# Conformer block on one core: the passage from attention over batch norm to FF2 rebuilt, softmax sums taken as one row, weight fold moved later

## Chip, cores, metric

One core of one Trainium2 chip. The metric is the time of one execution in device microseconds. Most runs of a kernel agree within 0.3%. Spans are from the profiled execution, which is about 4 us shorter than the time of the same execution (2103.5 against 2107.25 us).

Names: PE is TensorE, DVE is VectorE, ACT is ScalarE, POOL is GpSimd, SP is SyncE, whose queue issues most transfers. SBUF is the on-chip memory, PSUM the memory that matmuls write. FF1 and FF2 are the two feed-forward parts of the reference, pw1 and pw2 the products with `w_pw1` and `w_pw2`; the gate is `a * _sigmoid(b)`, swish is `_silu`. Warm matmuls are dummies whose result nobody uses; they run to keep PE's clock full.

## The reference, cut

```python
B, T, D, K = (2, 4000, 512, 3); F = 4 * D
h = _layernorm(x);  x1 = x + 0.5 * (_silu(h @ w_ff1_a) @ w_ff1_b)
h = _layernorm(x1); q, k, v = h @ w_q, h @ w_k, h @ w_v
p = _softmax(einsum('btd,bsd->bts', q, k) * scale)
x2 = x1 + einsum('bts,bsd->btd', p, v) @ w_o
h = _layernorm(x2) @ w_pw1; a, b = h[..., :D], h[..., D:]
h = a * _sigmoid(b)
dc = three-tap convolution of h along T, per channel
mu, var = mean and variance of dc over ALL B*T rows, per channel
dc = (dc - mu) / sqrt(var + 1e-05)
x3 = x2 + _silu(dc) @ w_pw2
x4 = x3 + 0.5 * (_silu(_layernorm(x3) @ w_ff2_a) @ w_ff2_b)
return _layernorm(x4)
```

The batch statistics need every row before any row can go on. That is the narrow place between attention and FF2: little work is ready there, and PE must be kept from standing still.

## The kernel before

The 8000 rows are 16 chunks of 500, each of 4 tiles of 125. Everything is kept in SBUF, bf16. PSUM is four S banks and four Y banks, each taken in turn. A helper records each operation and puts in the semaphore waits; engines work strictly in program order. `after(n, f)` runs f n steps later in the emission; one step is one block of FF1 or FF2, or one key tile in attention. Scores use M = Wq Wk^T and the output Wvo = Wv Wo, both computed once (the "fold") between FF1 matmuls. Attention is two matmul groups per key tile, scores (into S) and values (into Y), with values four tiles behind. The convolution of chunks 0 to 12 is done by DVE beside attention; chunks 13 to 15 come after it, as three diagonal matmuls ("depthwise").

The end of an attention chunk:

```python
def finish_queries(self, b, qc, done):          # called after the chunk's last value group
    for dc in range(DC):                        # clear the four Y banks: DVE 1, 3; ACT 0, 2
        ...
    S.op("DVE", ... tensor_copy(self.ahi, self.acc[s]))            # split of the f32 exp sums into two bf16 parts, hi ...
    S.op("DVE", ... tensor_tensor(out=self.alo, in0=self.acc[s], in1=self.ahi, op=ALU.subtract))  # ... and lo
    def sums():
        ps, b_ps = self.sbank()
        for ti in range(TPC):                   # 8 matmuls with ONE column each
            for part, bp in ((self.ahi, self.b_ahi), (self.alo, self.b_alo)):
                self.mm(ps[0:TILE, ti:ti + 1], part[:, ti * TILE:(ti + 1) * TILE], self.onec[:, 0:1], ...)
        S.op("DVE", ... reciprocal(self.rl[s], ps[0:TILE, 0:TPC]))
    self.after(1 if last else 2, sums)          # then 4 projections, residual by DVE with rl as scalar
```

The fold and its check (the flag says whether scores are bounded, so that exp needs no row maximum):

```python
self.after(6, self.fold_weights)                # counted from block 8 of FF1's first chunk
def fold_weights(self):
    ...                                         # 8 groups of 4 matmuls, one group per step
    def bound():
        S.op("DVE", ... tensor_reduce(self.nr1, self.nrm, AX.X, ALU.add))
        self.mm(ps[0:1, 0:1], self.nr1, self.onef, ...)      # PE waits for DVE here
        ...
    self.after(10, bound)
```

The passage, shortened: gate of chunk 14 and the last projections by steps; layer norm of chunk 15 with transposes by DMA; gate of 15 with depthwise 13 to 15; batch scale for all four channel blocks at once; twelve weight loads for FF2 from ACT's queue; then swish and pw2 of four chunks, each pw2 tile followed by a DVE residual, with the layer norm of chunk 0 in DVE's order after the first chunk; then FF2.

## Time and profile before

| | before |
|---|---|
| time, median of 4 (range) | 2109.22 us (2107.47 to 2110.82) |
| span of the profiled run | 2103.5 us |
| start to first attention group (q of the next chunk) | 461.13 us |
| from there to the last value groups ("the mark") | 1089.90 us |
| mark to first FF2 matmul | 66.83 us |
| first FF2 matmul to end | 485.64 us |

The four pieces add up to the span and are read from PE's timeline.

### The profile page before, as it was taken

What the parts mean: (1) busy time and instruction counts of PE and PEld (TensorE: products, weight loads), DVE (VectorE), ACT (ScalarE), POOL (GpSimd) and SP (SyncE); (2) the same over time, 40 slices, a digit from 0 to 9 for tenths busy, and PEclk for the clock granted to TensorE, in tenths of its full rate; (3) what the DMA queues carried; (4) which work ended last, traced back from release to release, by engine and by line L of the source; (5) the groups of instructions that cost most, each with busy time, mean ns of one, the idle gap of its engine ahead of it and who ended that gap; (6) DMA issues with size and microseconds to landing.
All of it is one profiled execution on the core that took longest, in us unless ns stands there. A gap on an engine that the chain in (4) does not pass through costs nothing.

```text
span 2103.5 us, 24444 instructions
## 1 busy us (share of the span) xinstructions
PE 2063.4 (98%) x9708; PEld 1040.7 (49%) x9710; DVE 1092.4 (52%) x2235; ACT 733.8 (35%) x1251; POOL 124.0 (6%) x260
## 2 busy tenths in 40 slices
PE   8999999999999999999999999999987999999998
PEld 4555555554444444444444444444443555555554
DVE  3345444324556566656665666566755344444433
ACT  3333333333333333333333333333325334434332
POOL 0111100000000000000000000000000000000000
PEclk9999999999999999999999999999999999999999
DMA  6222221110000000005300000000134011111111
GB/s 169 60 55 57 60 61 52 45 43 11 11 11 8 18 18 18 11 15 121 75 11 16 17 18 11 18 16 18 49 97 119 23 38 33 30 40 30 33 38 41
DMA packets 197262, 84.83 MB, mean 40 GB/s; under 512 B 145812, under 2 KB 196631, under 8 KB 197143
## 3 DMA queue, kind: packets, MB, share of 16 engines
q1 hardware_dynamic: 190567, 78.84, 15.2%
q10 hardware_dynamic: 6576, 4.38, 0.7%
q8 instruction: 78, 1.28, 0.3%
q14 instruction: 41, 0.34, 0.1%
HBM read 29.53 MB, written 19.04 MB: 23 GB/s over the span
## 4 chain that ended last, share of the span: by engine, by line
PE 94%; DVE 3%; SPq 1%; DMA 1%; ACT 1%; issue 0%; ACTq 0%; POOL 0%; POOLq 0%; DVEq 0%
PE s L458 54%; PE y L458 40%; DVE work L787 1%; SPq L491 1%; DVE work L792 1%; DMA xt<-in_x_dram 1%; DVE work L749 0%; ACT work L483 0%; DVE work L522 0%; DVE work L545 0%; DVE work L791 0%; ACTq L487 0%; SPq L487 0%; DMA keys<-in_w_o_dram 0%; POOL work L532 0%
## 5 line engine op out<-in xcount | busy, mean ns | idle before, releaser
L483 ACT ACTIVATE work<-s 128x500 bf16<-128x500 f32 (+2 forms) x1062 | 623.0, 587 | 1250.5 <-PE s L458 1240.4
L458 PE MATMUL s<-work,wff 128*128 128x500 bf16 x2560 | 629.8, 377 | 4.0 <-DVE wff L831 3.4
L458 PE MATMUL y<-work,keys 128*128 128x500 bf16 x2048 | 519.1, 374 | 1.2
L458 PE MATMUL s<-work,keys 128*128 128x500 bf16 x2048 | 517.4, 374 | 0.1
L458 PE MATMUL y<-wff,work 128*125 128x512 bf16 x2016 | 506.6, 379 | 0.0
L749 DVE TENSOR_TENSOR work<-work 128x500 f32<-128x500 f32 x496 | 334.7, 675 | 304.6 <-ACT work L483 302.8
L458 PEld LDWEIGHTS s<-work,wff 128*128 128x128 bf16 x2560 | 250.4, 98 | 284.1 <-DVE wff L831 3.9
L458 PEld LDWEIGHTS y<-wff,work 128*125 128x125 bf16 x2016 | 275.2, 137 | 173.5
L458 PEld LDWEIGHTS y<-work,keys 128*128 128x128 bf16 x2048 | 198.0, 97 | 244.3 <-DVE work L787 15.5
L458 PEld LDWEIGHTS s<-work,keys 128*128 128x128 bf16 x2048 | 199.2, 98 | 228.9 <-DVE work L678 0.6
L591 DVE SCALAR_TENSOR_TENSOR xt<-y,xt 125x512 bf16<-125x512 f32 x128 | 79.7, 682 | 369.2 <-PE y L458 369.2
L522 DVE BATCH_NORM_STATS2 work<-xt 125x6 f32<-125x512 bf16 x320 | 201.6, 679 | 9.4 <-DMA xt<-in_x_dram 9.3
L458 PE MATMUL s<-work 128*125 128x512 bf16 (+3 forms) x666 | 150.2, 349 | 22.2 <-DVE work L792 7.9
L532 POOL TENSOR_TENSOR work<-work 125x4 f32<-125x4 f32 x79 | 84.3, 1067 | 1147.9 <-DVE work L530 1147.9
L545 DVE TENSOR_SCALAR work<-xt,work 125x512 bf16<-125x512 bf16 x288 | 115.6, 447 | 21.5 <-POOL work L532 18.8
L458 PEld LDWEIGHTS s<-work 128*125 128x125 bf16 (+2 forms) x666 | 82.8, 137 | 76.5 <-issue 12.2
L591 DVE SCALAR_TENSOR_TENSOR xt<-s,xt 125x512 bf16<-125x512 f32 x64 | 43.7, 690 | 134.5 <-PE s L458 134.5
L831 DVE SCALAR_TENSOR_TENSOR wff<-wff,s 128x500 bf16<-128x500 f32 x64 | 43.2, 677 | 63.1 <-PE s L458 63.1
L483 ACT ACTIVATE wff<-s 128x500 f32<-128x500 f32 x64 | 37.6, 587 | 79.7 <-PE s L458 75.2
L591 DVE SCALAR_TENSOR_TENSOR xt<-s,work,xt 125x512 bf16<-125x512 f32 x64 | 48.1, 751 | 33.1 <-PE s L458 32.2
L458 PE MATMUL s<-keys,work 128*128 128x500 bf16 x256 | 64.4, 376 | 0.0
L483 ACT ACTIVATE work<-keys,work 128x500 bf16<-128x500 bf16 x64 | 49.6, 794 | 5.9 <-DMA wff<-in_w_ff_a_dram 3.7
(61 smaller groups left out, 420.8 us busy)
## 6 DMA issues: line engine op xcount, KB each, us to landing
xt<-in_x_dram SPq DMA_DIRECT2D x15, 500.0 KB
out_dram<-work SPq DMA_DIRECT2D x15, 500.0 KB
dcvd<-wff SPq DMA_DIRECT2D x52, 125.0 KB, 1.7
keys<-dcvd SPq DMA_DIRECT2D x13, 500.0 KB, 5.1
keys<-work SPq DMA_DIRECT2D x8, 512.0 KB, 3.6
keys<-keys SPq DMA_DIRECT2D x32, 128.0 KB, 2.3
work<-work SPq DMA_TRANSPOSE x188, 2.5
wff<-in_w_ff_a_dram SPq DMA_DIRECT2D x8, 256.0 KB, 5.3
```

What stands on the lines that cost most here:

```text
L458: self.S.op("PE", lambda e: e.matmul(out, lhsT, rhs, start=start, stop=stop), reads=reads, writes=[bank], inc=stop if inc is None else inc)
L483: return self.S.op("ACT", lambda e: e.activation(out, in_, func, **kw), reads=reads, writes=writes)
L491: return self.S.dma("SP", k, lambda e: e.dma_start_transpose(dst, src), reads=reads, writes=writes)
L522: self.S.op("DVE", lambda e: e.bn_stats(self.st[sl][:, ti, :], self.XT[g]), reads=[self.bx[g]], writes=[self.b_st[sl][ti]])
L532: S.op("POOL", lambda e: e.tensor_tensor(out=self.rs[sl], in0=self.va[sl], in1=self.neghalf[0:TILE, :], op=ALU.pow), reads=[self.b_va[sl], ...
L545: self.S.op("DVE", lambda e: e.tensor_scalar(out, self.XT[g], self.mv[sl][:, ti, 0:1], self.rs[sl][:, ti:ti + 1], ALU.subtract, ALU.mult), ...
L591: self.S.op("DVE", lambda e: e.scalar_tensor_tensor(out=self.XT[g], in0=ps, scalar=scalar, in1=self.XT[g], op0=ALU.mult, op1=ALU.add), rea ...
L749: S.op("DVE", lambda e, p=p: e.tensor_tensor(out=self.acc[s], in0=self.acc[s], in1=self.P[p], op=ALU.add), reads=[self.b_P[p], self.b_acc[ ...
L787: S.op("DVE", lambda e, dc=dc: e.tensor_copy(self.OT[:, dc, :], self.Yb[dc][:, 0:CHUNK]), reads=[self.b_Y[dc]], writes=[self.b_OT[dc]])
L792: S.op("DVE", lambda e: e.tensor_tensor(out=self.alo, in0=self.acc[s], in1=self.ahi, op=ALU.subtract), reads=[self.b_acc[s], self.b_ahi], ...
L831: self.S.op("DVE", lambda e: e.scalar_tensor_tensor(out=self.G[gs][:, jj, 1:1 + CHUNK], in0=self.th[k], scalar=1.0, in1=ps[:, 0:CHUNK], op ...
```

## The change

Five intentions: (1) sums as one row, with the split of the sums done before the last value groups; (2) fold later, so that its weights have landed; (3) ten more warm-up matmuls; (4) the passage reordered: gate of chunk 14 on ACT and POOL, PE transposes in place of DMA transposes, batch scale per channel block, residual of two chunks as an identity matmul on PE, 16 warm matmuls, FF2 loads from SP; (5) three instead of four chunks of pw2 ahead of FF2.

```diff
+                if kt == TB - 1:
+                    self.split_sums(s)              # ahi, alo: before the 4 lagging value groups
...
+    def sum_row(self, s):
+        ps, b_ps = self.sbank()
+        for part, bp in ((self.ahi, self.b_ahi), (self.alo, self.b_alo)):
+            self.mm(ps[0:1, 0:CHUNK], self.onec[:, 0:1], part, ...)      # 2 matmuls, 500 columns
+        self.act(self.row, ps[0:1, 0:CHUNK], AF.Copy, [b_ps], [self.b_row])
+        self.store(self.rowd[s:s + 1, :], self.row, ...)                 # row to DRAM
+        ... dma_start(self.sq[s], self.rowd[s].rearrange("(t p) -> p t", p=TILE))   # and back as columns
+        self.after(5, ... reciprocal(self.rl[s], self.sq[s]))
+    def finish_queries(self, g, done):
+        self.copy_o()
+        if g == NCK - 1: return
+        self.sum_row(g % 2)
...
     def conv_a(self, t, jj):
+        if t == NCK - 2:
+            self.act(asb, ps[:, 0:CHUNK], AF.Copy, [b_ps], [b_asb], scale=2.0)
+            self.S.op("POOL", ... tensor_tensor(out=out, in0=asb, in1=self.th[k], op=ALU.mult))
+        elif t == NCK - 1:
+            self.S.op("DVE", ... scalar_tensor_tensor(out=out, in0=ps[:, 0:CHUNK], scalar=2.0, in1=self.th[k], ...))
...
+    def pw2_sum(self, t, tiles, banks):
+            self.mm(ps[0:TILE, :], self.ident[0:TILE, 0:TILE], self.XT[g], True, False, ...)   # residual on PE
+            ... four pw2 matmuls ...
+            self.act(self.XT[g], ps[0:TILE, :], AF.Copy, [b_ps], [self.bx[g]])
...
-        self.warm(20)
+        self.warm(30)
-            self.after(6, self.fold_weights)
+            self.after(18, self.fold_weights)
...
+        self.sums_direct(last % 2)              # last chunk: the eight short matmuls
+        for ti in range(TPC):                   # gate groups of 14 between the projections of 15
+            gate.pop(0)(); self.project(last, ti); self.ln_stats(last, sl, ti)
+        self.ln_aggr(last, sl)
+        while gate: gate.pop(0)()
+        ... norms on DVE; self.transposes_pe(1, ("DVE", "DVE")); depthwise, gate of 15 interleaved
-            self.load_wa(i["w_ff2_a"], k, "ACT")
+            self.load_wa(i["w_ff2_a"], k)
-        AHEAD = 4
+        AHEAD = 3
+        self.warm(16)
+        ... pw2(0) with DVE residual; pw2_sum(1), pw2_sum(2); transposes of chunk 0 by PE
```

## The prediction

> **What bounds the kernel now.** I read the page first, then the waits of TensorE (PE), then the timeline in the three places where those waits sit.
>
> ```profile
> span 2103.5 us, 24444 instructions
> PE 2063.4 (98%) x9708; PEld 1040.7 (49%) x9710; DVE 1092.4 (52%) x2235; ACT 733.8 (35%) x1251; POOL 124.0 (6%) x260
> ...
> PE 94%; DVE 3%; SPq 1%; DMA 1%; ACT 1%; issue 0%; ACTq 0%; POOL 0%; POOLq 0%; DVEq 0%
> ```
>
> PE is the bound: 98% busy, and 94% of the chain that ended last. Only time in which PE does no useful matmul can be won. How much is that? In the last stretch of attention, 39 groups of four 128x500 matmuls start between 1516.36 and 1549.34 us: 32.98/156 = 0.2114 us per matmul. A chunk of FF1 (64 such matmuls and 64 of 125x512) repeats every 27.415 us, which leaves 0.217 us for a 125x512. The groups of the page hold 6948 of the first kind and (adding the 32 FF2 and 2 fold records that are missing) 2624 - 32 = 2592 of the second: 1468.8 + 562.5 = 2031 us. With the start (12.4 us before the first FF1 matmul) and the end (5.8 us after the last matmul) that makes 2050 us. Some 54 us of the 2103.5 are loss, more than the 40 us of PE idle, because a stalled or slowly clocked matmul counts as busy. No view shows a second place to win from.
>
> Loss one, in every attention chunk (timeline of the kernel before, PE, DVE):
>
> ```profile
> 1428.87 1.25 DVE L787 CAST work<-y 128x500 bf16<-128x500 f32 x2
> 1429.15 1.42 PE L458 MATMUL y<-work,keys 128*128 128x500 bf16 x4
> 1430.05 0.41 DVE L791 CAST work<-work 128x500 bf16<-128x500 f32 x1
> 1430.48 0.68 DVE L792 TENSOR_TENSOR work<-work 128x500 bf16<-128x500 f32 x1
> 1430.51 0.22 PE L458 MATMUL s<-work 128*125 128x1 bf16 x1
> 1431.22 0.56 PE L458 MATMUL s<-work 128*125 128x1 bf16 x7 [0.49 <-DVE work L792]
> 1431.64 1.01 PE L458 MATMUL s<-work,keys 128*128 128x500 bf16 x4
> ```
>
> A group of four takes 0.85 us elsewhere. Here the next chunk's first value group waits for VectorE (DVE) to clear the Y banks (starts 1429.15, next start 1430.51: 1.36), then the eight one-column sums wait for the hi/lo split that DVE does after those copies (0.71 + 0.42). Extra: 1.36 + 0.71 + 0.42 - 0.85 = 1.64 us. Check: a steady chunk repeats every 69.42 us and holds 304 x 0.2114 + 16 x 0.217 = 67.74, which leaves 1.68.
>
> Loss two, the weight fold in FF1's first chunk:
>
> ```profile
> 35.18 1.03 PE L458 MATMUL y<-wff,work 128*125 128x512 bf16 x4
> 37.43 0.81 PE L458 MATMUL s<-keys 128*128 128x512 bf16 x3 [1.22 <-DMA keys<-in_w_k_dram]
> ...
> 41.67 1.02 PE L458 MATMUL s<-keys 128*128 128x512 bf16 x4 [1.72 <-DMA keys<-in_w_o_dram]
> ```
>
> The fold waits for its weights, 1.22 + 1.72 = 2.9 us. Before that, at 12.4 to 15.3 us, seven FF1 matmuls come 0.42 apart: slow clock after the idle start, about 1.5 us.
>
> Loss three, the passage from attention to FF2:
>
> ```profile
> 1551.03 3.53 PE L458 MATMUL y<-work,keys 128*128 128x500 bf16 x16
> ...
> 1571.02 1.22 PE L458 MATMUL s<-work,wff 128*128 128x500 bf16 x4 [3.40 <-DVE wff L831]
> ...
> 1597.78 9.76 PE L458 MATMUL s<-work 128*125 128x512 bf16 x32 [7.67 <-ACT work L483]
> 1610.93 7.09 PE L458 MATMUL s<-work 128*125 128x512 bf16 x32 [3.39 <-DVE xt L591]
> 1617.86 4.41 PE L458 MATMUL s<-work,wff 128*128 128x500 bf16 x20
> ```
>
> From 1551.03 to the first FF2 matmul at 1617.86 are 66.8 us for 120 x 0.2114 + 80 x 0.217 + 0.4 = 43.2 us of matmuls. Loss: 23.7 us. The three long waits are layer norm of chunk 15 on DVE; batch statistics, the ACT table and twelve weight loads issued from ScalarE's own queue ahead of the first swish; and layer norm of chunk 0 standing in DVE's order ahead of a residual that holds a bank. Slow clock after each wait is the rest.
>
> **What the Trainium skill says.** "TensorE: Matmul & The Clock Gate", Part 1: a warm matmul starts every N/2.4 ns + about 2.5, i.e. 210.8 and 215.8 ns for 500 and 512 columns (measured here 211.4 and 217), and the clock halves after an idle window of some 3.4 us and comes back after a busy one. The trace agrees: 20 dummy matmuls ended at 7.4 us, FF1 began slowly at 12.4 and was fast from 15.28. "ScalarE: Activation LUTs", Table sets: exp and tanh share a set, sigmoid anchors another; a load is 1283 ns. The trace has three loads of 1283 ns, none between Exp and Tanh; the change adds one. "GPSIMD Engine Reference", 3.1: a two-input elementwise instruction takes about 2.6 cycles per element at 1.2 GHz. My estimate for 500 elements is 1.1 us and dispatch; the trace before has no such instruction. "DMA: Bandwidth & Descriptors", Anatomy of one DMA: about 2 us fixed per transfer (its fit is for another queue). Here 125 KB to DRAM landed in 1.7 us.
>
> **The change part by part.**
>
> *Sums as one row (15 of 16 chunks).* The split moves to the end of the chunk, before the four lagging value groups, so DVE has done it 6 us early. Eight one-column matmuls become two of 500 columns: 2 x 0.2114 = 0.42 us. These also stand between the last value group and the next chunk's first, so the Y copies get that much more time: the fourth matmul would now start at about 1430.2, and the copies above ended at 1430.12; the 0.5 us stall of the Y group shrinks to about 0. Gain per chunk 1.64 - 0.42 - 0.03 = 1.19; x15 = 17.8 us. The round trip of the row through DRAM (ScalarE copy 0.6, store about 2, load of 500 four-byte elements 3 to 4) ends roughly 7 us after the sums; its reciprocal is issued five steps later, about 7.9 us. If DVE waits there 1 or 2 us it costs nothing: DVE is busy 43.7 of 69.4 us per chunk, and eight P buffers and four S banks give it several us.
>
> *Later fold.* Same 32 matmuls, weights long landed: 2.9 us won. *Ten more warm matmuls* run at 0.21, to 9.5 us instead of 7.4, in idle time; whether they hold the clock until 12.4 depends on the window: half of 1.5, 0.7 us.
>
> *Passage.* I rescheduled it by hand from the durations above (DVE 0.6 to 0.75 per residual, stats or gate; ScalarE 0.59 per copy, 0.72 per swish; pow 1.0).
> - To 1554.4 values, sums 0.5, last values to 1555.8, gate group to 1556.65, projection waits 0.4 for the O copies; seven more groups alternate gate and projection to 1563.0; four gate groups to 1566.4. ScalarE and GpSimd take gate 14, so DVE is free: residual, stats, aggregate, pow end at 1566.3, norms follow. The 3.4 us wait becomes about 0.3.
> - Sixteen PE transposes paced by the norms to 1568.1, six depthwise matmuls to 1569.4 under their DVE copies. That replaces transposes by DMA.
> - Gate 15 and depthwise 13 to 15: 62 matmuls, 13.1 us, to 1582.5. DVE has about 15 us here (4 gates, 12 stats of 0.65, 4 aggregates of 0.6) and then the last scale chain: shift at 1587.0. Swishes run 1586.0 to 1591.7 because ScalarE's copies precede them. The 16 warm matmuls cover to 1586.
> - pw2 of chunk 0 ends at 1591.0 (pace of the swishes); chunks 1 and 2 with the residual as an identity matmul, 40 x 0.217 = 8.7, to 1599.6; layer norm of chunk 0 (DVE, done 1598.6) is hidden; transposes 1.4 and an eviction: FF2 starts at 1601.9.
>
> So 1617.9 - 1601.9 = 16.0 us; but pw2 of chunk 3 now runs inside FF2: 16 x 0.217 = 3.5 back. Net 12.5; I take 1 off for waits that I didn't see: 11.5.
>
> Sum: 17.8 + 2.9 + 0.7 + 11.5 = 32.9. From 2110.19: 2077.3, so 2077.
>
> **Rivals.**
> - *The row's round trip becomes the wait.* It is a chain of two dependent transfers of tiny elements. If it took 12 us rather than 7, DVE would stand 4 us in front of the residuals and the exp sums, P buffers would run out, and PE would lose perhaps 1 us per chunk: about 2092. For it: SyncE's queue is in order and carries the conv stores. Against: at that point the trace shows that queue free, and stores landing in 1.7 us.
> - *The passage stays bound by DVE and ScalarE.* The passage had only 40.0 us DVE and 26.2 us ScalarE in 66.9, so neither fills it, but between gate 15 and swish DVE is the longer one even in my schedule. A slow GpSimd multiply (3 us), or a cold clock for two windows, takes 3 to 6 us: about 2082.
> - *It gains as much as there is.* PE work of the new passage, with transposes, identity and warm matmuls, is 47.5 us: FF2 at 1598.5. With all of the 1.5 us at the start: 2071. So 2% (2068) is beyond what I can find to remove.
>
> **Range and chances.** Attention is 15 repeats of one well-read wait (17.8, give or take 2); passage 11.5, give or take 4; start 3.6, give or take 1; the three runs before spread over 3.4 us. Together 2069 to 2086. Faster by over 2% would need everything and the noise: 0.07. Slower by 2% needs a new wait of over 70 us: 0.01. Within 2%: 0.92.
>
> **What would show it.** Steady chunks every 68.2 us instead of 69.4, with two 128x500 matmuls where the eight were, no DVE release there; no DMA release in the first 60 us; first FF2 matmul 51 us, give or take 4, after the mark from which 66.8 were counted above, no wait over 2.5 us in the passage. I am wrong if reciprocals wait long for their DMA and PE follows, if DVE or ScalarE still leaves PE over 4 us idle ahead of pw2, or if the chunk period stays at 69.

## The result

| | before | after | gain | predicted |
|---|---|---|---|---|
| median of 4 | 2109.22 | 2080.02 (2079.44 to 2083.02) | ratio 0.9865 [0.9848, 0.9882] | 2077 |
| span | 2103.5 | 2076.1 | 27.4 | 32.9 |
| start to attention | 461.13 | 460.71 | 0.4 | 3.6 |
| attention to mark | 1089.90 | 1074.29 | 15.6 | 17.8 |
| mark to FF2 | 66.83 | 51.91 | 14.9 | 15 (16.0 less 1) |
| FF2 to end | 485.64 | 489.19 | -3.5 | -3.5 |

Two rows were missed: the start gave almost nothing, and attention gave 2.2 us less. The passage came as predicted in sum. The gain is clear of the noise but under 2%, the least that counts here as faster.

The page of the kernel after, engine totals and the chain that ended last (shares by engine):

```profile
PE 2060.9 (99%) x9684; PEld 1040.1 (50%) x9686; DVE 1088.8 (52%) x2235; ACT 748.5 (36%) x1282; POOL 126.7 (6%) x267
...
PE 97%; DVE 1%; ACT 0%; issue 0%; DMA 0%; POOL 0%; POOLq 0%; SPq 0%
```

PE is still the bound, more than before. Its waits (line, for whom, total us, times, longest):

```profile
PE s L467 <- DVE work L1053: 2.8, 1, 2.8
PE s L483 <- DVE work L560: 2.4, 3, 1.2
PE s L467 <- ACT work L498: 2.0, 4, 0.8
PE s L467 <- DVE work L1071: 1.7, 1, 1.7
PE s L467 <- DVE work L490: 0.6, 1, 0.6
```

The 16 waits for the split, the two for the fold's weights and the 7.7 us ahead of swish are gone. One is new and the longest: 2.8 us for line 1053, which is the `tensor_reduce` of the bound check. The sums in attention (timeline after, PE and DVE):

```profile
1413.50 1.00 PE L467 MATMUL y<-work,keys 128*128 128x500 bf16 x4
1414.43 0.58 PE L467 MATMUL s<-work 128*1 128x500 bf16 x2
1414.95 1.02 PE L467 MATMUL s<-work,keys 128*128 128x500 bf16 x4
1415.81 1.00 PE L467 MATMUL y<-work,keys 128*128 128x500 bf16 x4
...
1423.99 0.17 DVE L837 RECIPROCAL work<-work 125x4 f32<-125x4 f32 x1
```

The value group at 1415.81 runs through in 1.00 instead of 1.42 us and no DVE wait is left, as predicted. The reciprocal starts without a wait, in all 15 chunks, so the trip through DRAM is hidden. But from value group to value group (1413.50 to 1415.81) are 2.31 us against the usual 1.69: the row costs 0.62, not 0.45. The period is 68.39 us (1414.43 to 1482.82), 1.03 less than before, and 15 x 1.03 = 15.5.

The passage (timeline after, PE, the starts of its stages):

```profile
1535.00 3.54 PE L467 MATMUL y<-work,keys 128*128 128x500 bf16 x16
...
1551.26 1.03 PE L483 MATMUL s<-work 125*128 125x125 bf16 x12 [1.20 <-DVE work L560]
1553.16 0.38 PE L483 MATMUL s<-work 125*128 125x125 bf16 x4 [0.87 <-DVE work L560]
...
1572.01 0.40 PE L467 MATMUL s<-work 128*125 128x512 bf16 x1 [0.70 <-ACT work L498]
...
1586.91 3.35 PE L467 MATMUL s<-work,wff 128*128 128x500 bf16 x15 [0.81 <-ACT work L498]
```

No wait is over 1.2 us where there had been 3.4, 7.7 and 3.4. But from 1567.8 to 1572.0 PE runs only the 16 warm matmuls and then waits 0.7 us: 4.2 us without useful work, until ScalarE's swishes come (PE idled 7.7 us there before). So the prediction's second rival, a passage still bound by DVE and ScalarE, holds in part; its schedule had counted on such a stretch (warm matmuls from 1582.5 to 1586).

### The profile page after: what moved, and what is told of

It reads as the page before. It is cut to its first block, busy times and chain, and to the rows that moved or that the text cites. A ratio compares the mean times of both kernels' runs of the same rounds, so it can differ in the third digit from the quotient of the medians. Undisturbed runs are those within 1.5% of the kernel's fastest.

```text
span 2076.1 us, 24427 instructions
## 1 busy us (share of the span) xinstructions
PE 2060.9 (99%) x9684; PEld 1040.1 (50%) x9686; DVE 1088.8 (52%) x2235; ACT 748.5 (36%) x1282; POOL 126.7 (6%) x267
## 3 DMA queue, kind: packets, MB, share of 16 engines
q8 instruction: 78, 1.28, 0.3%
## 4 chain that ended last, share of the span: by engine, by line
PE 97%; DVE 1%; ACT 0%; issue 0%; DMA 0%; POOL 0%; POOLq 0%; SPq 0%
PE s L467 55%; PE y L467 42%; DVE work L537 0%; DVE wff L954 0%; DMA xt<-in_x_dram 0%; DVE work L560 0%; DVE xt L606 0%; ACT work L498 0%; ACT keys L498 0%; DVE wff L888 0%; ACT wff L498 0%; POOL work L547 0%; DVE work L490 0%; PE s L483 0%; DVE work L961 0%
## 5 line engine op out<-in xcount | busy, mean ns | idle before, releaser
L498 ACT ACTIVATE work<-s 128x500 bf16<-128x500 f32 (+3 forms) x1077 | 631.5, 586 | 1221.7 <-PE s L467 1212.0
L467 PE MATMUL s<-work 128*125 128x512 bf16 (+4 forms) x586 | 148.7, 377 | 5.7 <-DVE work L1053 2.8
L547 POOL TENSOR_TENSOR work<-work 125x4 f32<-125x4 f32 x79 | 80.0, 1013 | 1186.7 <-DVE work L545 1186.7
L606 DVE SCALAR_TENSOR_TENSOR xt<-s,xt 125x512 bf16<-125x512 f32 x56 | 38.7, 691 | 141.6 <-PE s L467 141.6
L467 PEld LDWEIGHTS s<-work 128*125 128x125 bf16 (+3 forms) x586 | 74.6, 131 | 61.1 <-ACT work L498 7.3
L892 DVE SCALAR_TENSOR_TENSOR wff<-wff,s 128x500 bf16<-128x500 f32 x56 | 38.0, 678 | 74.1 <-PE s L467 74.1
```

Of the source, the lines that this page charges most:

```text
L467: self.S.op("PE", lambda e: e.matmul(out, lhsT, rhs, start=start, stop=stop), reads=reads, writes=[bank], inc=stop if inc is None else inc)
L498: return self.S.op("ACT", lambda e: e.activation(out, in_, func, **kw), reads=reads, writes=writes)
L547: S.op("POOL", lambda e: e.tensor_tensor(out=self.rs[sl], in0=self.va[sl], in1=self.neghalf[0:TILE, :], op=ALU.pow), reads=[self.b_va[sl], ...
L606: self.S.op("DVE", lambda e: e.scalar_tensor_tensor(out=self.XT[g], in0=ps, scalar=scalar, in1=self.XT[g], op0=ALU.mult, op1=ALU.add), rea ...
L892: self.S.op("DVE", lambda e: e.scalar_tensor_tensor(out=out, in0=self.th[k], scalar=1.0, in1=ps[:, 0:CHUNK], op0=ALU.add, op1=ALU.mult), r ...
```

## The experiments

Twelve kernels, all with correct results. Labels beginning with a or c start from the kernel after, those with b from the kernel before. Only a1 and c1 were timed in five rounds; the others are one look each, and their verdicts rest on the timeline of the profile, not on the time.

### Where did the fold's gain go?

The timeline after, around the new wait:

```profile
75.39 2.48 DVE L606 SCALAR_TENSOR_TENSOR xt<-y,xt 125x512 bf16<-125x512 f32 x4 [20.92 <-PE y L467]
77.79 2.46 DVE L537 BATCH_NORM_STATS2 work<-xt 125x6 f32<-125x512 bf16 x4
80.17 0.14 DVE L1053 TENSOR_REDUCE work<-work 128x1 f32<-128x4 f32 x1
80.46 0.19 PE L467 MATMUL s<-work 128*1 128x1 f32 x2 [2.76 <-DVE work L1053]
80.58 1.85 PE L467 MATMUL s<-work,wff 128*128 128x500 bf16 x4
82.23 1.71 PE L467 MATMUL y<-wff,work 128*125 128x512 bf16 x4
```

The check comes 10 steps after the fold. With the fold 12 steps later it lands just behind the end of FF1's second chunk, where DVE has four residuals and four statistics in its order ahead of the tiny reduction. PE waits 2.76 us for one number that nobody needs before the end of the program, and the eight matmuls after it come at half speed (3.2 us for eight).

**a1_bound_late** (after, one number):

```diff
-        self.after(10, bound)
+        self.after(20, bound)
```

> The changed kernel with one number changed: the score-bound check after the weight fold comes 20 steps after its start instead of 10. Theory (the fold's gain was given back at the bound check): PE's 2.76 us wait at 80.5 us and the slow clock after it (8 matmuls at 0.42, 1.7 us) go; the first attention group moves from 460.9 to about 456.5 us, span 2076.1 to about 2071.7. Rival (the weights' wait was never on the path, the start is bound by something else such as loads of x): attention still starts at 460.5 to 461, span 2076.

Measured: attention starts at 456.64 us, span 2071.7 (up to 2073.3 in the other four runs), median of 5 2077.0 us, ratio to before 0.9842 [0.9828, 0.9855]. In the profiled run the theory's numbers hold to 0.2 us and the rival is out: the weights' wait had been on the path, and its gain was handed back at the check.

**b1_fold_only** (before):

```diff
-            self.after(6, self.fold_weights)
+            self.after(18, self.fold_weights)
```

> The kernel before with only the fold 12 steps later. Theory: the two waits for weights (2.9 us) go, but the bound check now falls behind four residuals and four statistics in DVE's order and costs 2.8 us of wait and about 1.7 us of slow clock: span 2103.5 to about 2105, attention start about 462.8 instead of 461.3. Rival (the collision comes from the ten more warm matmuls or chance): span about 2100.6, attention start 458.4.

Measured (timeline, PE):

```profile
81.74 0.19 PE L458 MATMUL s<-work 128*1 128x1 f32 x2 [2.76 <-DVE work L973]
```

PE waits 2.76 us for the same reduction, attention starts at 462.21 (461.13 before). So the later fold by itself is a loss of 1.1 us; the collision needs neither the warm matmuls nor the passage. The span, 2106.7, contains 2 us more of passage (68.88 from mark to FF2), which no part of this edit touches; see the clock under b2.

**b2_warm_only** (before):

```diff
-        self.warm(20)
+        self.warm(30)
```

> The kernel before with only 30 instead of 20 warm matmuls. Theory: the clock stays full until FF1, which is 1.4 us ahead at 15 us, but the fold's matmuls then wait that much longer for weights whose landing doesn't depend on PE (second fold group at about 41.5 us in either case): attention start 461.3 plus or minus 0.3, span 2103.5. Rival (the two gains add as I predicted): attention start about 460, span 2102.

Measured: the clock stays full at FF1's first matmuls (20 in 4.41 us), and the fold then waits once, 2.04 us, for its weights (1.22 and 1.72 before) and runs at about half speed after it. Attention starts at 460.52: 0.6 us gained, between my theory (0 plus or minus 0.3) and the rival (1.3), and outside the theory's range. The span is longer, 2107.3, because in this run more of the passage ran at the slow clock, the second half of pw2 above all (2.7 us), and the projections after the sums (16 matmuls in 4.88 us instead of 3.62):

```profile
1598.48 10.15 PE L458 MATMUL s<-work 128*125 128x512 bf16 x32 [7.25 <-ACT work L483]
1612.02 9.83 PE L458 MATMUL s<-work 128*125 128x512 bf16 x32 [3.39 <-DVE xt L591]
```

In the kernel before the lines were 9.76 and 7.09 us long. After the same waits the clock is sometimes kept and sometimes not; from mark to FF2 the unchanged passage took 66.8, 68.9, 71.3 and 65.0 us in before, b1, b2 and b3 (b3 changes how it begins). The profile of before is on the fast side, and the runs of that kernel spread over 6.4 us (2105.73 to 2112.13 in nine runs).

### What did the row bring?

**b3_split_early** (before; the sums stay short and late):

```diff
+                if kt == TB - 1:
+                    ... ahi = acc; alo = acc - ahi          # on DVE, before the lagging value groups
-        (the same two operations in finish_queries)
```

> The kernel before with only the hi/lo split of the exp sums moved to the end of its chunk; the eight one-column sum matmuls stay where they were. Theory (of the 1.64 us lost per chunk, 0.6 to 0.7 is the wait for the split, 0.5 the wait of the value group for the Y copies, 0.43 the sums themselves): period 69.42 to 68.75 us, 15 to 16 chunks, span about 2093. Rival (the one-row form is what matters, and the split's wait is only passed on): period 69.2 or more, span 2100 or more.

Measured: period 68.62 us (1351.21 to 1419.83), span 2089.6. Its timeline:

```profile
1418.57 1.42 PE L458 MATMUL y<-work,keys 128*128 128x500 bf16 x4
1419.83 0.57 PE L458 MATMUL s<-work 128*125 128x1 bf16 x8
1420.26 1.01 PE L458 MATMUL s<-work,keys 128*128 128x500 bf16 x4
```

0.80 of the 1.03 us per chunk come from emitting two DVE instructions earlier. I had expected 0.67: the value group's start-to-start also fell, from 1.36 to 1.26. The value group still stalls on the Y copies (1.42). In the passage, too, the waits for the last chunk's sums (1.50 and 0.50 us before) are gone, so up to 2 us of what the passage gained belong to the early split.

**a2_sums_direct** (after):

```diff
-        self.sum_row(g % 2)
+        self.sums_direct(g % 2)
```

> The changed kernel with the eight one-column sum matmuls back in place of the row (at the row's place, split early), so without the trip through DRAM. The row adds 0.62 us per chunk (value group at 1413.50, next one at 1415.81 in the profile: 2.31 against 1.69), not the 0.45 predicted. Theory (the row costs its two full-length matmuls and some lost weight prefetch): eight short ones cost 0.43 to 0.55, period 68.39 to 68.2 or 68.3, span 1.5 to 2.9 us shorter, 2073.2 to 2074.6. Rival (the row form itself is the gain): period 68.6 or more, span 2079 or more.

Measured: period 68.20 us (1342.62 to 1410.82), attention 1071.5 instead of 1074.3 us, span 2072.2. As the theory had it, the short sums at the row's place (eight in 0.43 us, 1410.82 to 1411.25; the row's two take 0.52) are cheaper than the row by 0.19 us per chunk, 2.8 us in all, and need no transfer, no ScalarE copy and no buffer. (The other 1.1 us of the span's 3.9 are from the start: after the wait at the bound check the clock stayed full in this run.) So the row form is no part of the gain; the early split (0.80 us per chunk in b3) and the place, between the last value group and the next score (0.42 more, b3's period against a2's), are.

### What carries the passage?

All of these start from the kernel after, where mark to FF2 is 51.91 us.

**a3_gate_half** and **a4_gate_dve**:

```diff
-        if t == NCK - 2:                       # a3: and jj < 2;  a4: never
+        if t == NCK - 2 and jj < 2:
...
-        elif t == NCK - 1:
+        elif t >= NCK - 2:
```

> The changed kernel with the gate of chunk 14's last two blocks on DVE instead of ScalarE and GpSimd. In the profile after, the four norms of chunk 15 took 3.21 us beside two GpSimd multiplies; four such norms took 1.38 without. Theory (GpSimd multiply and DVE norm disturb each other): norms take 1.4 us again, but start about 1.1 us later behind the two gates; transposes end about 0.7 earlier, first FF2 matmul 0.5 to 1 us earlier than 51.9 us after the last value groups begin. Rival (the norms are slow for another reason): norms still about 3 us, FF2 later by 1 us.

> The changed kernel with all four gates of chunk 14 on DVE. If the disturbance eats what GpSimd relieves: aggregate 2 us later, norms 1.4 us long, first FF2 matmul 0 to 1.5 us later than after (51.9 to 53.4 from the mark). If taking the gate off DVE is what removed the 3.4 us wait, as predicted: 3 us later or more (55 or more).

Measured: 51.01 us in both, 0.9 earlier than after. In the kernel after, the norms lie beside the multiplies (timeline, POOL and DVE), in a4 they don't:

```profile
1549.72 1.24 POOL L885 TENSOR_TENSOR wff<-wff 128x500 bf16<-128x500 f32 x1
1549.79 3.21 DVE L560 TENSOR_SCALAR work<-xt,work 125x512 bf16<-125x512 bf16 x4 [1.12 <-POOL work L547]
1551.44 1.43 POOL L885 TENSOR_TENSOR wff<-wff 128x500 bf16<-128x500 f32 x1
```

```profile
1550.99 1.37 DVE L560 TENSOR_SCALAR work<-xt,work 125x512 bf16<-125x512 bf16 x4
```

Four norms take 3.21 us beside two GpSimd multiplies and 1.37 without. Asked for in shorter stretches, the first and the last of the four take 1.32 and 1.33 us, each ending about 0.15 us after a multiply does (1550.96 and 1552.87), and the two between take 0.4: a norm mostly stands still while a multiply runs. DVE's residual and statistics beside the multiply at 1543.15 keep their 0.75 and 0.70 us. a3 did what its theory said. a4 was to be 0 to 1.5 us slower than after, and is 0.9 faster. The idea behind the gate's move, freeing DVE ahead of the norms, does not pay: PE waits 1.26 us in a4 with DVE doing all four gates, against 1.20 + 0.87 in after. So the old 3.4 us wait was cut by something else in the passage. The traces point to the order on DVE. In the kernel before PE waits for a gate of chunk 14 (line 831), which stands in DVE's order behind the residuals, statistics and norms of chunk 15:

```profile
1568.99 1.38 DVE L545 TENSOR_SCALAR work<-xt,work 125x512 bf16<-125x512 bf16 x4 [1.12 <-POOL work L532]
1570.29 1.26 DVE L831 SCALAR_TENSOR_TENSOR wff<-wff,s 128x500 bf16<-128x500 f32 x2
```

In a4 the four gates stand between the residuals (1543.24, 1546.60) and ahead of the norms (1549.05, 1550.39, norms at 1550.99), and no gate group of PE waits. b3 has the early split with the old order and keeps the wait (3.41 us), so the split did not remove it. The order was not undone alone.

**a5_no_warm16**:

```diff
-        self.warm(16)
```

> The changed kernel without the 16 warm matmuls ahead of pw2. Theory: PE idles 4.2 us there, the clock falls to half[...], FF2 starts 1.5 to 3.5 us later (53.4 to 55.4 from the mark). Rival (the idle stretch is short enough, or falls across two windows): within 0.5 us of 51.9.

Measured: 52.86 us, 0.95 later, outside both ranges. PE idles 4.08 us and the 16 pw2 matmuls of chunk 0 take 5.49 us, part of them slow. The warm matmuls are worth about 1 us here. Since the clock is sometimes kept and sometimes not after like waits (b2), one run doesn't fix its size.

**a6_residual_dve**:

```diff
-        self.pw2_sum(1, ...); self.pw2_sum(2, ...)
+        self.pw2(1, ...); self.pw2_residual(1, ...)
         (norms of chunk 0, moved up to here)
+        self.pw2(2, ...); self.pw2_residual(2, ...)
```

> The changed kernel with the residual of pw2 for chunks 1 and 2 added by DVE again, not by an identity matmul on PE and a copy on ScalarE (norms of chunk 0 put between the two). Saves 8 matmuls, 1.7 us of PE, and adds 8 x 0.69 = 5.5 us to DVE. Theory (DVE is what PE waits for there): first FF2 matmul 2 to 4 us later than 51.9 from the mark. Rival (PE is the bound there): 1 to 1.7 us earlier.

Measured: 53.67 us, 1.8 later, and 20 matmuls of FF2 then take 6.59 instead of 4.41 us (slow clock after a wait of 2.75 us for DVE), so 3.9 us in all. The rival is out. The theory's range held for the sum, and the start of FF2 alone fell just under it.

**a7_dma_transposes**:

```diff
-        self.transposes_pe(1, ("DVE", "DVE"))
+        for ti in range(TPC): self.transpose(self.lnT[1][:, ti], self.ltm[ti], ...)      # DMA
```

> The changed kernel with chunk 15's transposes by DMA again (as in the kernel before) instead of by PE with DVE copies. PE saves 1.4 us and DVE 1.4, but four transposes issue one after another, 1.27 us each, and land 2.5 us later; only six depthwise matmuls (1.27 us) cover it. Theory: first FF2 matmul 2 to 4 us later. Rival (the order alone was the gain): within 1 us of 51.9.

Measured: 57.10 us, 5.2 later, more than expected: PE waits 6.44 us for the last transfer and the next eight matmuls take 3.49 us at the slow clock (1.86 in after):

```profile
1558.04 3.49 PE L467 MATMUL s<-work,wff 128*128 128x500 bf16 x8 [6.44 <-DMA work<-work]
```

**a8_loads_on_act**:

```diff
-            self.load_wa(i["w_ff2_a"], k)                # and the same for the other FF2 loads
+            self.load_wa(i["w_ff2_a"], k, "ACT")
```

> The changed kernel with the twelve FF2 weight loads issued from ScalarE's queue again, as before the change. In the profile before, ScalarE spent 5 us issuing them between the last depthwise matmul and the first swish. Theory: first swish and pw2 3 to 6 us later, FF2 3 to 6 us later than 51.9. Rival (batch statistics, not the issues, held the first swish): within 1 us.

Measured: 60.51 us, 8.6 later, again more than expected. ACT's timeline:

```profile
1568.73 3.70 ACTq L502 DMA_DIRECT2D wff<-in_w_ff_a_dram  x5
1572.48 0.59 ACT L498 ACTIVATE keys<-y 128x500 bf16<-128x500 f32 x1 [3.17 <-DVE wff L954]
...
1574.26 4.15 ACTq L502 DMA_DIRECT2D wff<-in_w_ff_b_dram  x4
1578.46 2.19 ACT L498 ACTIVATE work<-keys,work 128x500 bf16<-128x500 bf16 x3 [4.44 <-DMA wff<-in_w_ff_a_dram]
```

The first group of loads holds up depthwise copies, the last holds up the first swish, which starts at 1578.46 us: 43.1 from the mark, against 36.1 in after (1571.08). PE idles 6.26 us, goes cold, and pw2 of chunk 0 takes 6.09 instead of 3.5 us (16 x 0.217). In this setting the queue the loads are issued from is the largest single item that I undid in the passage. (The undone parts don't add: 8.6 + 5.2 + 1.8 + 1.0 - 0.9 is more than the 14.9 won.) Four parts of the passage were not undone alone: the order on DVE, the batch scale per channel block, the statistics read from PSUM ahead of ScalarE's copy, and three chunks ahead instead of four.

### The corrected kernel

**c1_all** is the kernel after with a1, a2 and a4 together, and ScalarE evicting every second PE transpose.

```diff
-        self.transposes_pe(1, ("DVE", "DVE"))
+        self.transposes_pe(1, ("DVE", "ACT"))          # and the edits of a1, a2, a4
```

> The changed kernel with the three corrections together: bound check at 20 steps (alone 4.4 us of span), direct short sums instead of the row (2.6 us of attention), gate of chunk 14 all on DVE (0.9 us of passage), and ScalarE, now free there, evicting every second PE transpose (0.3 to 0.7). If they add: span 2076.1 - 4.4 - 2.6 - 0.9 - 0.5 = 2067.7, ratio to before about 0.982. Rival (they share a wait): span 2070 or more.

Measured: median of 5 2072.08 us (2071.75 to 2072.20), span 2068.1, ratio to before 0.9825 [0.9812, 0.9839]. Start to attention 456.35, attention 1071.53, mark to FF2 50.96, FF2 to end 489.26: the three corrections add. The eviction by ScalarE brought 0.05 us, not 0.3 to 0.7. The slowest run of c1 (2072.20 us) is faster than every run of both kernels; its five runs lie within 0.45 us, where nine runs of before spread over 4 to 6.4.

## Why the prediction was right or wrong, point by point

- *PE is the bound and only its loss can be won.* Right. PE's share of the chain rose from 94 to 97%.
- *Sums: 1.19 us per chunk, 17.8 in all.* Mechanism right, size off: 1.03 and 15.6. The mis-sized term is "two of 500 columns: 2 x 0.2114 = 0.42", with 0.03 for the rest; the row costs 0.62. In the timeline the row's first matmul starts 0.09 us after the slot it could have had (1414.43 against 1413.50 + 0.845) and the two with the switch to the next group take 0.52. The weight loads of both groups start together with their first matmul there instead of 0.2 us ahead; that this is the cause was not tested. I also credited the row form with what the early split does: b3 has 0.80 of it, a2 beats the row.
- *Y-bank stall shrinks to 0.* Right: 1.42 to 1.00 us.
- *Row's trip through DRAM hidden; the rival that it becomes the wait.* Right, and the rival is refuted: no reciprocal waited. The load was issued 1.15 us after the store (1415.70 and 1416.85).
- *Later fold: 2.9 us.* This is the step that failed. "Same 32 matmuls, weights long landed" looked at what the fold waits for, and not at the check that moves along with it. The check is a chain DVE to PE, and its new place was behind DVE's busiest order. Moving the fold won the wait and gave 2.8 us of new wait and 1.5 us of slow clock back (attention at 460.71 in after, 456.64 in a1); a1 and b1 show both halves.
- *Ten more warm matmuls: 0.7.* They do keep the clock to FF1 (20 matmuls in 4.41 instead of 5.76 us). That is 1.35 us, twice the 0.7. It adds to the fold's gain only once the fold no longer waits for its weights: alone the warm matmuls gained 0.6 us (b2). In c1 the start gains 4.8 us over before, where I had 3.6.
- *Passage: 11.5 net.* 14.9 - 3.5 = 11.4, so right in sum, with an error inside that another covered. My schedule had FF2 at 1601.9, 50.9 from the mark, and c1 stands at 50.96. Against it, after loses about 1 us beside the GpSimd multiplies: the step "ScalarE and GpSimd take gate 14, so DVE is free: ... The 3.4 us wait becomes about 0.3" failed. It became 1.2 + 0.9, and 1.26 without the gate's move (a4). DVE was free as early as thought (pow ended 14.8 us after the mark, 15.3 in the schedule); what failed is "norms follow", which took 3.21 us. The reading of the old wait as "layer norm of chunk 15 on DVE" also left out that PE waited for a gate standing behind it. The 1 us that I took off "for waits that I didn't see" was about this size by luck.
- *Loads, transposes, residual off DVE.* That these belong to the gain is shown by a8, a7 and a6. I had counted the loads as a wait of ACT's queue, but gave neither them nor the transposes a size of their own; both are larger than I would have said (8.6 and 5.2).
- *The rival "It gains as much as there is".* Its own terms give 17.8 + 2.9 + 1.5 + 19.4 - 3.5 = 38.1 and 2072, 1 us more than its 2071. c1 came to 2072.08 with another split: 4.8 at the start, 18.4 in attention, 12.3 net in the passage. (In the count of matmuls the 32 FF2 records are added and taken off again; 2592 is right.)
- *Range and chances.* The measured 2080.02 us lies inside the range and within 2%, which had 0.92, 3 us above the middle; the misses are 3.2 us at the start and 2.2 in attention. The runs of before lie on average above its profiled one, which made the measured difference of medians 29.2 rather than 27.4.

## What to carry to other kernels

When a piece of work is moved in time, move in thought everything that hangs on it, down to the smallest reduction: a one-number chain between engines costs what stands in the queue ahead of it, not what it computes. Before changing the form of a step that waits, try emitting its input earlier; here two instructions moved gave most of what a new data path gave. An engine is not free help if the one it relieves stands still beside it, and a PE gap can cost twice, once as idle time and once as slow clock after it.

## What the Trainium skill lacked or had wrong

- "TensorE: Matmul & The Clock Gate", Part 1, gives PE gaps over about 3.4 us as what lets the clock fall. Here shorter gaps were followed by slow matmuls: 2.04 us at the fold in b2, and 2.75 to 2.76 us at the bound check in after, a4, a7, a8 and b1; after the same gap they stayed fast in a2, a3, a5 and a6. Attention starts at 459.1 to 459.7 in the four that stayed fast and at 460.7 to 461.1 in after, a4, a7 and a8, against 456.4 to 456.6 with the check moved (c1, a1). The page says that its window runs free, which fits an outcome that varies for the same gap, but not that a gap shorter than the window is enough. (The prediction's "The trace agrees" passed over this: before FF1's slow start the longest gap is 2.77 us.)
- "GPSIMD Engine Reference", 3.1, has no figure for what a GpSimd instruction costs beside its 2.6 cycles per element. At 1.2 GHz these are 1.08 us for 500 elements, an estimate; the two-input 128x500 multiply takes 1.24 to 1.25 us, and 1.43 where a norm of DVE was running as it began. (The page's Specifications say that SBUF interfaces are shared with VectorE for some of VectorE's instructions. The trace agrees: norms stand still beside a multiply, residuals and statistics don't.)
- "DMA: Bandwidth & Descriptors", Anatomy of one DMA, has about 2 us fixed, fitted for another queue. The figure doesn't carry over to SP's queue: a 2000-byte row stored to DRAM had landed early enough for a dependent load to be issued 1.15 us after the store, where the prediction took 2.
- "ScalarE: Activation LUTs", What ACT_TABLE_LOAD costs, has 1283 ns and a drain of 1380 ns. The added load (Exp to Sigmoid) takes 1.28 us, starts 0.01 us after the last exp ends (1535.26 + 0.59, load at 1535.86), and the next activation starts 0.02 us after its end (1537.16): no drain is seen there.
